# A list scheduler for the middle of a three-stage kernel: gated linear attention, then two feed-forward layers

## The chip, the cores and the metric

The kernel runs on one core of a Trainium2 chip. A core has TensorE (PE in the profile, its weight loads PEld), VectorE (DVE), ScalarE (ACT), GpSimd (POOL) and SyncE (SP, which here issues every DMA). Each engine takes its own instructions strictly in the order of its queue and waits for the others by semaphores. The metric is the time of one execution on the device in microseconds; lower is better.

## The reference

Three stages follow each other; the output of one is the input of the next.

```python
# 1: attention, 4 batches x 8 heads, 768 tokens, head size 48
state = f[t][:, None] * state + outer(k[t], v[t])      # f = sigmoid(f_logit)
y[t] = q[t] @ state
# 2: x is y as 3072 tokens x 384
h = x @ w_in                                           # 384 -> 2048
x = (h * sigmoid(1.702 * h)) @ w_out                   # 2048 -> 384
# 3: four experts, each 384 -> 1024 -> 384
p = probs / (probs.sum(-1) + 1e-9)
out = sum(p[:, e] * (maximum(x @ w1[e], 0) @ w2[e]) for e in range(4))
```

All of it is float32. The kernel reaches this with products of split numbers: a number is a rounded part ("hi", type fp32r) and the rest ("lo", its low half), and hi x hi + hi x lo + lo x hi are summed, so each product is three matmuls.

## The kernel before, in words

**Attention** goes in 24 chunks of 128 tokens (`attend`, line 521). For a chunk DVE, POOL and ACT make the forget gates (tanh, then a scaling, "g"), two scans over time on DVE (lines 547 and 553), and scaled k and q; PE transposes k (line 563), multiplies k by q (scores, line 569), updates the state (line 598) and makes outputs (line 637); masks are applied to the scores (lines 582 and 587).

**The first MoE** (stage 2) goes in 6 blocks of 512 tokens; block j needs the chunks 4j to 4j+3. A block has 16 steps, one for 128 of the 2048 inner columns. Step part L is 9 matmuls (line 679), then come tanh on ACT (685), the gelu product on DVE (687), the hi copy on ACT (469) and the low half on DVE or POOL (471); part M is 9 matmuls of the second product (697) into three banks that collect the whole block, two steps behind L. At the end of a block its sums are taken out of the banks (`sums_out`) and stored to `ydram`.

**The second MoE** (stage 3) uses a fast bilinear scheme, on blocks of 3x3 tiles of x and of w1: `FORM_Y` gives 15 sums of blocks of x, `FORM_W` 15 sums of w1 blocks, and `FORM_H` puts 15 products together. It goes in 32 units n (16 blocks of the experts' inner columns, for each half of the tokens); a unit has 15 products (`p_task`, line 1076) and then, two units later in PE's order, 9 second products U with w2 (`u_task`, line 1116), whose results are multiplied by p on DVE (1129) and added up on POOL (1131).

The weights of stage 3 are prepared during stage 2. `w_forms` loads a 128x1536 block of w1, makes 12 sums on POOL (777) and 15 hi and low halves (786 to 790), and stores them to `wfd`, one 256-column piece per store (794). `w2_piece` loads a third of a w2 block, splits it on ACT (808) and POOL (809) and stores both halves to `w2d` (810, 811). The second MoE loads them back from `wfd` and `w2d`.

**What sets the order.** There are three regimes. `startup` (attention of the chunks 0 to 11 and blocks 0 and 1, with the split of w_in and w_out) follows a list written out by hand, `ORDER`. The loop from line 1291 on (blocks 2 to 4, chunks 12 to 23, all `w_forms` and `w2_piece`) hands out its instructions step by step from a table, `at(i, fn)`, and is outside `manual_schedule`, so that the program's own scheduler may move instructions on the queues; in the trace the first w1 load is issued at 155.83 us, inside the startup. The last block and the second MoE go through `Plan`: each piece of work is a `Task` with an engine, an estimated duration and a delay until others see its result; PE's tasks run in the order of their `place`, and on the other engines, SP included, `order` picks again and again the task that can begin first by these estimates. Buffers come from pools (`F`, `W1`, `W2`, `G`, `S`, `Y`, `TM`, ...), and a task that needs one begins when a slot is free.

## Time and profile before

| | us |
|---|---|
| median of 3 runs (1334.80 to 1340.93) | 1338.81 |
| the profiled execution | 1339.19 |
| its span, first to last instruction | 1337.5 |
| PE busy | 1249.2 (93%) |
| DVE busy | 975.6 (73%) |
| POOL busy | 691.2 (52%) |
| ACT busy | 515.5 (39%) |

"Busy" is the time that an engine's own records cover. PE's matmuls overlap one another, so a busy PE can still run below its best pace; PEclk is the clock granted to it, as a share of 2.4 GHz. The mean over the span is 0.971.

### The profile page before, as it was taken

The page shows a single profiled execution, that of the slowest core. Times are in us where ns is not written, and L with a number is a line of the kernel's source. Part 1 is how long each engine was busy: PE and PEld are TensorE (multiplying, and loading weights), DVE is VectorE, ACT ScalarE, POOL GpSimd, SP SyncE. Part 2 cuts the span into 40 slices and gives each one's busy share as a digit, 9 for nine tenths or more (in the row PEclk, how much of TensorE's full clock was granted, in tenths as well). Part 3 has the DMA queues.
Part 4 walks back from the last instruction along what each step waited for, and adds up shares of the span by engine and source line. Part 5 has one row for each costly group of instructions (what it writes and reads, how often), then busy time and mean ns, then how long its engine had stood idle before and what let it go on. Part 6 is the DMA issues. An engine that isn't in the chain of part 4 may idle for free.

```text
span 1337.5 us, 20734 instructions
## 1 busy us (share of the span) xinstructions
PE 1249.2 (93%) x7470; PEld 1026.9 (77%) x7470; DVE 975.6 (73%) x1443; ACT 515.5 (39%) x967; POOL 691.2 (52%) x591
## 2 busy tenths in 40 slices
PE   6699999987987889899999999999999999999988
PEld 5698877766866767687888888888778888888877
DVE  7989757776767655857777777778977777777774
ACT  4576634444444443333232323233332323232322
POOL 5857434553345442700888555555515555555542
PEclk6899999999989989899999999999999999999989
DMA  6654326776766668144767344436773444353473
GB/s 189 177 149 135 106 92 186 237 245 186 239 211 198 216 196 302 52 154 140 254 207 230 120 129 137 131 121 200 185 194 121 141 130 141 108 159 112 132 154 108
DMA packets 158657, 221.51 MB, mean 166 GB/s; under 512 B 49776, under 2 KB 100048, under 8 KB 158544
## 3 DMA queue, kind: packets, MB, share of 16 engines
q1 hardware_dynamic: 158544, 220.09, 53.7%
q8 instruction: 60, 0.98, 0.3%
q14 instruction: 53, 0.43, 0.1%
HBM read 158.91 MB, written 61.13 MB: 165 GB/s over the span
## 4 chain that ended last, share of the span: by engine, by line
PE 66%; DVE 11%; DMA 10%; issue 5%; POOL 5%; ACT 2%; SPq 1%; DVEq 0%; ACTq 0%; POOLq 0%
PE bank L1116 25%; PE bank L1076 23%; PE bank L697 6%; PE bank L679 5%; DMA wfd<-cv 3%; PE bank L1166 2%; POOL wide L777 2%; PE bank L893 1%; PE bank L637 1%; DMA cv<-in_w 1%; DVE cv L787 1%; DVE arena L553 1%; DMA w2d<-cv 1%; PE bank L569 1%; DVE r L938 1%
## 5 line engine op out<-in xcount | busy, mean ns | idle before, releaser
L1131 POOL TENSOR_TENSOR arena<-arena 128x512 f32<-128x512 f32 x252 | 358.9, 1428 | 270.9 <-DVE arena L1129 270.3
L1076 PE MATMUL bank<-r,r 128*128 128x512 f32 x1440 | 376.9, 391 | 9.9 <-DVE arena L1093 8.2
L1076 PEld LDWEIGHTS bank<-r,r 128*128 128x128 f32 x1440 | 269.9, 188 | 69.9 <-DVE arena L1093 11.9
L1116 PE MATMUL bank<-r,r 128*128 128x512 f32 x876 | 273.9, 389 | 0.0
L1129 DVE TENSOR_TENSOR arena<-bank,cv 128x512 f32<-128x512 f32 x252 | 173.2, 688 | 112.4 <-PE bank L1116 106.7
L1116 PE MATMUL bank<-g,r 128*128 128x512 f32 x744 | 242.9, 389 | 0.0
L679 PE MATMUL bank<-r,r 128*128 128x512 f32 (+1 forms) x792 | 190.5, 386 | 20.0 <-DVE arena L687 19.2
L1116 PEld LDWEIGHTS bank<-r,r 128*128 128x128 f32 x876 | 164.7, 188 | 34.4
L697 PE MATMUL bank<-g,r 128*128 128x512 f32 (+1 forms) x774 | 181.7, 379 | 7.7 <-ACT cv L708 5.2
L679 PEld LDWEIGHTS bank<-r,r 128*128 128x128 f32 x792 | 140.8, 194 | 52.4 <-DVE arena L687 22.8
L697 PEld LDWEIGHTS bank<-g,r 128*128 128x128 f32 x774 | 138.5, 193 | 37.4 <-ACT cv L708 6.0
L1116 PEld LDWEIGHTS bank<-g,r 128*128 128x128 f32 x744 | 139.8, 188 | 29.1
L1093 DVE TENSOR_TENSOR arena<-arena,bank 128x512 f32<-128x512 f32 x192 | 130.1, 683 | 31.4 <-ACT arena L1089 22.8
L1089 ACT ACTIVATE arena<-bank 128x512 f32<-128x512 f32 x101 | 60.4, 598 | 108.6 <-PE bank L1076 107.8
L1100 ACT ACTIVATE r<-arena 128x512 fp32r<-128x512 f32 x75 | 47.1, 632 | 131.7 <-DVE arena L1093 131.7
L777 POOL TENSOR_TENSOR wide<-wide 128x256 f32<-128x256 f32 x64 | 54.9, 874 | 59.0 <-DMA wide<-in_w 33.4
L687 DVE SCALAR_TENSOR_TENSOR arena<-arena,bank 128x512 f32<-128x512 f32 (+1 forms) x88 | 54.9, 626 | 33.1 <-ACT arena L685 30.9
L1093 DVE TENSOR_TENSOR wide<-wide,bank 128x512 f32<-128x512 f32 x96 | 65.6, 683 | 17.7 <-ACT wide L1089 12.2
L469 ACT CAST g<-arena 128x512 fp32r<-128x512 f32 (+1 forms) x88 | 50.9, 581 | 63.4 <-DVE arena L687 62.9
L471 DVE TENSOR_TENSOR g<-arena,g 128x512 fp32r<-128x512 f32 (+1 forms) x66 | 57.5, 871 | 22.9 <-ACT g L469 22.2
L809 POOL TENSOR_TENSOR cv<-cv,cv 128x512 f32<-128x512 f32 x24 | 33.0, 1375 | 73.0 <-ACT cv L808 59.7
L787 DVE TENSOR_TENSOR cv<-wide,cv 128x256 f32<-128x256 f32 x72 | 41.4, 584 | 33.3 <-ACT cv L786 33.1
(140 smaller groups left out, 1562.8 us busy)
## 6 DMA issues: line engine op xcount, KB each, us to landing
r<-wfd SPq DMA_DIRECT2D x160, 384.0 KB, 3.1
wfd<-cv SPq DMA_DIRECT2D x120, 256.0 KB, 2.7
r<-w2d SPq DMA_DIRECT2D x64, 384.0 KB, 4.1
w2d<-cv SPq DMA_DIRECT2D x48, 256.0 KB, 2.3
wide<-ydram SPq DMA_DIRECT2D x38, 256.0 KB, 4.1
arena<-in_qkf SPq DMA_DIRECT2D x48, 192.0 KB, 4.3
arena<-in_v SPq DMA_DIRECT2D x24, 256.0 KB, 4.2
wide<-in_w_in SPq DMA_DIRECT2D x12, 512.0 KB, 3.7
```

The source lines that it names most:

```text
L471: eng.tensor_tensor(out=lo, in0=src, in1=hi.bitcast(F32), op=ALU.subtract)
L679: nc.tensor.matmul(h, w[:, c0:c0 + 128], x[:, 512 * k + t0:512 * k + t0 + n], start=(i == 0), stop=(i == 8),)
L687: nc.vector.scalar_tensor_tensor(out=gf, in0=th, scalar=1.0, in1=h, op0=ALU.add, op1=ALU.mult)
L697: nc.tensor.matmul(bank[d][:, t0:t0 + n], w[:, c0:c0 + 128], g, start=(f == fs[0] and i == 0 and t0 == 0), stop=(f == fs[-1] and i == 2 an ...
L777: nc.gpsimd.tensor_tensor(out=t, in0=have[a], in1=have[b], op=ALU.add if sg > 0 else ALU.subtract)
L787: nc.vector.tensor_tensor(out=lo, in0=fv, in1=hl[:, :, 0], op=ALU.subtract)
L1076: nc.tensor.matmul(bk.ap, a, y.ap, start=(r == chain[0] and m == 0), stop=(m == 2), skip_group_check=True,)
L1089: P.task("ACT", act, lambda: nc.scalar.activation(out=b.ap, in_=bk.ap, func=ACTF.Copy, scale=float(sign)), [bk], [b])
L1093: P.task("DVE", dve, lambda: nc.vector.tensor_tensor(out=b.ap, in0=b.ap, in1=bk.ap, op=ALU.add if sign > 0 else ALU.subtract), [b, bk], [b])
L1116: nc.tensor.matmul(bk.ap, w.ap[:, c0:c0 + 128], g[f][y].ap, start=(m == 0), stop=(m == 5))
L1129: P.task("DVE", dve, lambda: nc.vector.tensor_tensor(out=m.ap, in0=bk.ap, in1=pb.ap, op=ALU.mult), [bk, pb], [m])
L1131: P.task("POOL", pool, lambda: nc.gpsimd.tensor_tensor(out=a.ap, in0=a.ap, in1=m.ap, op=ALU.add), [a, m], [a])
```

## The change

Four things are done together.

1. `Plan` also takes blocks 2 to 4, the chunks 12 to 23, the w1 sums, the experts' probabilities and the test of the decay (`guard`). The table `at`, `w2_piece` and the unplanned loop go. In the plan a chunk starts with step i (`chunk_steps`: 0, 3, 6, 10, ... 42); PE makes its transposes and scores after the L of step i+3, its update and outputs after that of step i+4 (one later still for the first chunk). The w1 blocks start at the steps `w_at`: 2, 7, 13, 19, 25, 30, 36, 42.
2. The scheduler is extended. A task may have several ways (`other`): the low half of a step, k and q of a chunk and the positive w1 low halves can go to DVE or POOL, and the second way is taken when it would end no later by the estimates. Tasks have a `rank` that decides between tasks that can begin at the same time (w1 work has 2). Pools hold places made of cells, so that one piece of memory can serve several pools. All masks of chunks 12 to 23 become an ACT copy and a POOL select; in the kernel before they are one DVE product each.
3. The w1 halves of three forms are collected in one tile of 1536 columns (`WG`, two of them), and each tile goes out in two stores of 384 KB (80 stores in all; 120 of 256 KB before).
4. w2 is not split in stage 2 and `w2d` is gone. `load_w2` reads two 128x384 pieces of w2 for each unit into slots of the pool `Y` and splits them on ACT and POOL, beside the unit's products.

The memory for the gates, `FG`, moves to the end of the arena, the block sums of blocks 2 to 4 go through the pool `TM` (the slots of tanh and gelu product), and the terms of `later_forms` are loaded one by one, each after its own mark.

```diff
+                for w in t.ways:
+                    known = max([d.end + (d.late if d.engine != w[0] else 0.0) for d in t.deps], default=0.0)
+                    begin = max(known, free.get(w[0], 0.0), place)
+                    if w is not t.ways[0] and begin + w[1] > max(known, free.get(t.ways[0][0], 0.0), place) + t.ways[0][1]:
+                        continue
+                    key = begin, t.rank, known, t.n
...
-        P.pool("S", [*(asl(i) for i in range(9, 14)), slot(0), slot(1), slot(2)], free=6.0)
-        P.pool("Y", [slot(3), slot(4), slot(5)])
-        P.pool("TM", [asl(i) for i in range(14, 18)])
+        P.pool("S", [*(a_slot(i) for i in range(9, 12)), *(b_slot(i) for i in range(5))])
+        P.pool("TM", [a_slot(i) for i in range(12, 16)])
+        P.pool("WT", [b_slot(3 + i // 2, i % 2) for i in range(6)])
+        P.pool("Y", [b_slot(5), b_slot(12), b_slot(13)])
+        P.pool("WG", [(CV3[i], [("b", 6 + 3 * i + x // 2, x % 2) for x in range(6)]) for i in range(2)])
...
+            P.task("POOL", 1.4, lambda: nc.gpsimd.tensor_tensor(out=t[:, 2], in0=t[:, 2], in1=pc, op=ALU.mult), [Q, PCB], [Q],
+                   other=[("DVE", 0.85, lambda: nc.vector.tensor_tensor(out=t[:, 2], in0=t[:, 2], in1=pc, op=ALU.mult))])
...
+                P.task("ACT", 0.62, lambda g=g, dst=dst: nc.scalar.copy(
+                    out=dst, in_=sb[g].ap.rearrange("p (h t) -> p h t", h=4)), [sb[g]], [am_b[g]])
+                P.task("POOL", 1.1, cover, [am_b[g]], [am_b[g]])
...
-            P.task("DVE", dve, lambda: nc.vector.tensor_tensor(
-                out=lo.ap, in0=gf.ap, in1=hi.ap.bitcast(F32), op=ALU.subtract), [gf, hi], [lo])
+            P.task("DVE", 0.8, lambda: nc.vector.tensor_tensor(
+                out=lo.ap, in0=gf.ap, in1=hi.ap.bitcast(F32), op=ALU.subtract), [gf, hi], [lo],
+                other=[("POOL", 1.5, lambda: nc.gpsimd.tensor_tensor(
+                    out=lo.ap, in0=gf.ap, in1=hi.ap.bitcast(F32), op=ALU.subtract))])
...
+                    P.task("ACT", 0.42, hi, [bs], [h], rank=2)
+                    P.task("DVE", 0.53, lo, [bs, h], [l], rank=2, other=[
+                        ("POOL", 0.95, lambda lo=lo: lo(eng=nc.gpsimd))] if sign > 0 else ())
+                for i in range(2):
+                    stored["w", 2 * u + i, g] = dma(393216, lambda i=i, g=g, tile=tile: [(
+                        wfd[2 * u + i, g], tile.ap[:, 768 * i:768 * i + 768])], parts)
...
+        for i in range(n_last + 16):
+            s, place = early + i, 10.0 * i - 1e6
+            l_task(s, place)
+            wait.append(s)
+            if i in chunk_steps:
+                x = 1 if i == 0 else 0
+                going[i] = att_task(chunk_steps[i], [place + 32 + 10 * x, place + 42 + 10 * x, place + 43 + 10 * x])
...
+            if i in w_at:
+                w_forms(w_at[i], [P.te[-1][2]] if i > 2 else [])
...
+            if len(wait) > 2:
+                m = wait.pop(0)
+                m_task(m, place + 5)
+                if m % 16 == (early + 15) % 16 and m < early + n_last + 15:
+                    sums((m - early) // 16 + 2)
+        attended = next(t for t in reversed(P.tasks) if t in x_b[1][0][3].writers)
...
         for k, t in need:
-            y_load(raws[k, t], t, k)
+            y_load(raws[k, t], t, k, [attended])
...
-                    b.ap.bitcast(F32)[:, 768 * x:768 * x + 768].rearrange("p (f c) -> p f c", f=2),
-                    w2d[u, x].rearrange("p (f i c) -> p i f c", f=2, i=2)[:, i],
-                ) for x in range(2)]
-            dma(786432, go, (), [b], after)
+            for f in range(2):
+                r = Buf("Y")
+                f0 = DM * (2 * f + i)
+                after = [dma(196608, lambda r=r, f0=f0: [(r.ap[:, 0:DM], w2[u][:, f0:f0 + DM])], (), [r],
+                             [*after, *last2])]
+                last2[:] = after
+                h, l = (lambda f=f, x=x: b.ap[:, 768 * x + DM * f:768 * x + DM * f + DM] for x in range(2))
+                P.task("ACT", 0.48, lambda r=r, h=h: nc.scalar.copy(out=h(), in_=r.ap[:, 0:DM]), [r], [hi])
+                P.task("POOL", 1.15, lambda r=r, h=h, l=l: nc.gpsimd.tensor_tensor(
+                    out=l(), in0=r.ap[:, 0:DM], in1=h().bitcast(F32), op=ALU.subtract), [r, hi], [lo])
...
-                later_forms([marks[x // 2 + 2, 7 * (x % 2)] for x in range(20)])
+                later_forms([marks[x // 2 + 1, 7 * (x % 2)] for x in range(22)])
...
-        for i in range(e):
-            for fn in side.pop(i, []):
-                fn()
-            L1(early + i)
-            if len(pend) > 2:
-                L2()
-        plan = second_moe()
-        done = plan.order()
+        done = second_moe().order()
         with tc.manual_schedule():
             for t in done:
                 t.fn()
```

## Rows read from the trace of the kernel before

**Rows 1.** Page, part 2: busy tenths of PE in 40 slices of 33.4 us.

```profile
PE   6699999987987889899999999999999999999988
```

**Rows 2.** Windows by stage: length, busy us by engine, PEclk, DMA share, GB/s.

```profile
200.00:222.29 22.29, 19.45 (x224) 15.27 (x224) 20.02 (x32) 11.56 (x25) 12.79 (x15) 1.00 0.52 161
222.29:515.86 293.57, 255.02 (x2033) 203.20 (x2032) 198.63 (x324) 132.89 (x291) 131.22 (x149) 0.95 0.70 221
515.86:601.08 85.22, 78.52 (x326) 62.09 (x325) 55.05 (x69) 30.22 (x53) 30.98 (x21) 0.96 0.43 147
601.08:920.00 318.92, 318.48 (x1402) 262.70 (x1401) 237.44 (x343) 96.56 (x159) 187.96 (x134) 1.00 0.52 166
920.00:1000.00 80.00, 75.80 (x327) 60.47 (x326) 72.01 (x104) 31.00 (x53) 30.59 (x21) 1.00 0.71 184
```

**Rows 3.** Timeline of PE, 438 to 453 us: start, duration, instructions.

```profile
438.13 2.21 PE L679 MATMUL bank<-r,r 128*128 128x512 f32 x9
440.18 2.21 PE L697 MATMUL bank<-g,r 128*128 128x512 f32 x9
...
452.34 0.85 PE L697 MATMUL bank<-g,r 128*128 128x512 f32 x3
```

**Rows 4.** Lines, 222 to 516 us: count, busy us, mean ns, idle before.

```profile
L679 PE MATMUL bank<-r,r 128*128 128x512 f32 x432 | 115.0, 412 | 17.6 <-DVE arena L687 17.6
L697 PE MATMUL bank<-g,r 128*128 128x512 f32 x416 | 107.0, 400 | 7.7 <-ACT cv L708 5.2 <-DVE cv L706 0.8 <-DVE g L471 0.8
...
L809 POOL TENSOR_TENSOR cv<-cv,cv 128x512 f32<-128x512 f32 x23 | 31.1, 1353 | 72.1 <-ACT cv L808 58.9 <-DMA arena<-in_qkf 6.7 <-DMA wfd<-cv 6.6
```

**Rows 5.** Waits, 222 to 516 us: who for whom, total, times, longest.

```profile
PE bank L679 <- DVE arena L687: 17.6, 8, 5.9
...
PE bank L637 <- DVE arena L587: 8.5, 5, 2.9
```

**Rows 6.** Timeline of all engines, 376 to 385 us.

```profile
377.99 0.62 POOL L538 TENSOR_SCALAR arena<-arena 128x512 f32<-128x512 f32 x1
...
379.05 1.26 POOL L809 TENSOR_TENSOR cv<-cv,cv 128x512 f32<-128x512 f32 x1
...
379.22 2.17 DVE L547 TENSOR_TENSOR_SCAN arena<-arena,floor 128x512 f32<-128x512 f32 x1
...
383.18 0.67 DVE L687 SCALAR_TENSOR_TENSOR arena<-arena,bank 128x512 f32<-128x512 f32 x1
...
383.91 1.65 PE L679 MATMUL bank<-r,r 128*128 128x512 f32 x3 [5.88 <-DVE arena L687]
```

**Rows 7.** Timeline of POOL and DVE, 549 to 558 us.

```profile
549.80 1.74 POOL L959 TENSOR_TENSOR wide<-arena 128x512 f32<-128x512 f32 x1
550.32 1.77 DVE L938 TENSOR_TENSOR r<-arena,r 128x512 fp32r<-128x512 f32 x1
...
551.50 1.74 POOL L959 TENSOR_TENSOR arena<-arena 128x512 f32<-128x512 f32 x1
```

**Rows 8.** Line 471, DVE, 222 to 516 us: ns min/median/max.

```profile
L471 DVE TENSOR_TENSOR g<-arena,g x47: 675/693/1786, 227.8 to 515.0; 128x512 fp32r<-128x512 f32 x47
```

**Rows 9.** Line 1131 on POOL, whole span: ns min/median/max.

```profile
L1131 POOL TENSOR_TENSOR arena<-arena x252: 1277/1295/1759, 640.2 to 1299.6; 128x512 f32<-128x512 f32 x126
```

**Rows 10.** Line 1180 on POOL, the same columns.

```profile
L1180 POOL TENSOR_TENSOR arena<-arena x9: 1011/1017/1062, 1298.6 to 1318.2; 128x384 f32<-128x384 f32 x9
```

**Rows 11.** Page, part 6: DMA issues, KB each, median us to landing.

```profile
wfd<-cv SPq DMA_DIRECT2D x120, 256.0 KB, 2.7
...
arena<-in_qkf SPq DMA_DIRECT2D x48, 192.0 KB, 4.3
```

**Rows 12.** Chain that ended last, 516 to 560 us: start, us, what.

```profile
519.68 5.08 DMA arena<-ydram
...
524.78 5.38 DMA arena<-ydram
...
530.23 6.61 DMA ydram<-arena
```

More of the change, by code (lines that the diff above doesn't have):

```diff
@@ L98, with __init__ @@
 class Buf:
[L99 to L100 removed]
+    def __init__(self, pool=None, whole=None):
+        self.pool, self.place, self.whole = pool, None, whole
         self.writers, self.readers, self.refs = [], [], []
+        self.left, self.till = 0, 0.0
     @property
     def ap(self):
[L105 to L117 removed]
+        return (self.whole or self).place[0]
 class Task:
[L121 to L122 removed]
+    def __init__(self, ways, late, deps, rank):
+        self.ways, self.late, self.deps, self.rank = ways, late, deps, rank
+        self.engine, self.us, self.fn = ways[0]
         self.begin = self.end = None
@@ L129, in __init__, with pool, hold, at @@
     def __init__(self):
-        self.tasks, self.pools, self.te = [], {}, []
-    def pool(self, name, aps, free=0.0):
-        self.pools[name] = [Slot(a, free) for a in aps]
-    def hold(self, name, slots, buf):
-        for i in slots:
-            self.pools[name][i].held = buf
-        buf.slot = self.pools[name][slots[0]]
-        return buf
-    def task(self, engine, us, fn, reads=(), writes=(), after=(), late=0.1, place=None):
+        self.tasks, self.pools, self.te, self.holds = [], {}, [], {}
+    def pool(self, name, places):
+        self.pools[name] = places
+    def hold(self, buf, cells, ap=None):
+        for c in cells:
+            self.holds[c] = buf
+        buf.place = ap, cells
+        return buf
+    def at(self, place):
+        t = 0.0
+        for c in place[1]:
+            b = self.holds.get(c)
+            if b is not None:
+                if b.left:
+                    return None
+                t = max(t, b.till)
+        return t
+    def task(self, engine, us, fn, reads=(), writes=(), after=(), late=0.1, place=None, rank=0, other=()):
         deps = list(after)
@@ L146, in task @@
             deps += b.readers + b.writers
-        t = Task(engine, us, late, fn, list(dict.fromkeys(deps)))
-        t.bufs = list(dict.fromkeys(list(writes) + list(reads)))
+        t = Task([(engine, us, fn), *other], late, list(dict.fromkeys(deps)), rank)
+        t.bufs = list(dict.fromkeys(b.whole or b for b in [*writes, *reads]))
         for b in writes:
@@ L169, in order @@
                 d.users.append(t)
-        ready = {t.engine: [] for t in self.tasks}
         for t in self.tasks:
-            if not t.left and t.engine != "PE":
-                ready[t.engine].append(t)
+            for b in t.bufs:
+                b.left += 1
+        ready = [t for t in self.tasks if not t.left and t.engine != "PE"]
         done, k = [], 0
@@ L189, in order @@
             if best is None:
                 raise ValueError("no task can begin")
-            (begin, _, _), t = best
+            (begin, _, _, _), t, (t.engine, t.us, t.fn) = best
             for b in t.bufs:
-                if b.slot is None:
-                    free_slots = [s for s in self.pools[b.pool] if s.at() is not None]
-                    s = min(free_slots, key=lambda s: s.at())
-                    s.free, s.held = s.at(), b
-                    b.slot = s
+                if b.place is None:
+                    open_ = [p for p in self.pools[b.pool] if self.at(p) is not None]
+                    self.hold(b, (p := min(open_, key=self.at))[1], p[0])
@@ L198, in order @@
             t.begin, t.end = begin, begin + t.us
+            for b in t.bufs:
+                b.left -= 1
+                b.till = max(b.till, t.end + t.late)
             free[t.engine] = t.end
@@ L202, in order @@
             else:
[L203 removed]
+                ready.remove(t)
             done.append(t)
@@ L842, in second_moe, with r_part, a_slot, b_slot @@
-        old = {r: P.hold(*held(r), Buf(held(r)[0])) for r in range(20) if r not in (16, 17)}
+        def r_part(r, n, i):
+            w = 1536 // n
+            return R[r][:, w * i:w * i + w], [("r", r, x) for x in range(6 // n * i, 6 // n * (i + 1))]
+        def a_slot(i):
+            return asl(i), [("a", i)]
+        def b_slot(i, h=None):
+            if h is None:
+                return slot(i), [("b", i, 0), ("b", i, 1)]
+            return slot(i)[:, 256 * h:256 * h + 256], [("b", i, h)]
@@ L948, in y_load @@
             rows = yrows[j]
+            after = [*after, *(stored[r, k] for r in rows if (r, k) in stored)]
             dma(262144, lambda: [(buf.ap, ydram[rows[0], k])], (), [buf], after)
```

468 lines of the change are left out of this document (266 added, 202 removed).

## The prediction, made before the change was run

> **What bounds the kernel now.** The profiled execution took 1339.19 us (span 1337.5 and 1.7 around it), 0.4 above the median of the three runs, 1338.81; the sum below is made on the span and put on 1339.2. I read the page's forty slices first. TensorE is busy in nine tenths of nearly every slice, but slices 8 to 16 fall to seven or eight [rows 1]. The windows by stage turn this into places: from 601 to 920 us, the second MoE under its planner, PE is busy 318.48 of 318.92 us at full clock, so an order there can give nothing; from 222.29 to 515.86, blocks 2 to 4 with attention and the w1 sums beside them, 255.02 of 293.57, at a mean clock of 0.95; from 515.86 to 601.08, the planned last block, 78.52 of 85.22 [rows 2].
>
> Busy is not pace, so I price PE's work by distances between starts. A group of nine matmuls follows another after 2.04 us. From 438.13 to 452.34 PE did five groups and one whole chunk of attention (transposes, scores, state update, outputs) with no stall: 14.21 less 5 x 2.04 leaves 4.0 us a chunk [rows 3]. Between 222.29 and 515.86 stand 48 first-product groups and 46 second-product groups [rows 4] and chunks 12 to 23, two of them without a state update (0.45 each): 94 x 2.04 + 12 x 4.0 - 0.9 + 0.5 for two small transposes = 239.4 us. The stage took 293.6, so it **loses 54.2**. From 515.86 to 601.08 there are 34 groups and 18 product matmuls (about 4.4 us): 73.8 of 85.2, a **loss of 11.4**. Together 65.6 us, 45.3 of it idle PE and the rest groups at a lower clock; this is all that ordering can return.
>
> Why it loses: PE waits for the gelu product on DVE (L687, 17.6 us in 8 waits, the longest 5.9) and for masks on DVE (L587) [rows 5]. One of them in time: POOL does the gate of a chunk at 377.99, behind two w1 sums; POOL then splits w2 at 379.05, and the DVE scan of 379.22, which had to wait for the gate, is stretched to 2.17; the gelu product that PE needs stands behind it on DVE and runs at 383.18, PE at 383.91 after 5.88 us idle [rows 6]. That is a matter of queue order, not of a full engine: DVE is busy 198.6 and POOL 131.2 of 293.6 us [rows 2].
>
> **The change, part by part.** *Queue order in blocks 2 to 5.* All 64 steps, twelve chunks, eight w1 blocks and the sums go through the list scheduler. PE's order is written out: transposes and scores of a chunk stand three steps after its start instead of two, updates and outputs together a step later, so DVE's chain of scans has about a step (4.1 us) more. All the other queues are filled by who can begin first. The instructions that PE runs are the same, so its floor stays 239.4 + 73.8. What stays lost is the question, and the trace has two planned stages for it: 0.1% (601 to 920) and 13% (11.4 of 85.2). On 239.4 us these are 0.3 and 32. The mix here has the scans and POOL work which the first lacks, and less than the burst of the second; I take **20**, somewhat above the middle, for the reason in the next paragraph.
>
> *The pair DVE and POOL.* 24 masks go from DVE to ACT and POOL, and the low halves may go to POOL. Against it stands how they run together: from 549.80 to 551.50 each POOL operation starts 1.70 after the one before, one DVE operation between, and both take 1.7 [rows 7], while the same DVE operation alone takes 0.69 [rows 8] and POOL's 1.29 [rows 9]: 1.70 is 0.86 of the sum, so they run nearly one after the other. I add up what has two operands in SBUF on DVE and all of POOL, at undisturbed durations x 0.86 (small shapes estimated by width from these rows): 48 low halves 28, scans and k of 12 chunks 35, 120 w1 halves 42, 96 w1 sums 62, POOL's five parts of 12 chunks 39: 206 of 239 us, 86%. That is below PE, but not far; moving 10 low halves adds 5. Hence 20 and not 10. The Trainium skill states this as a rule (SBUF — State Buffer, "Who interferes with whom": a DVE instruction with two SBUF inputs and a GpSimd one that reads SBUF shut each other out for a whole instruction), and Perfetto Trace Analysis, "Optimizing Scalar/DVE Operations", adds that offloading between those two might not help. By that the offload is worth nothing or less; the first rival below is what it would do here.
>
> *w2's split.* Out of the stage go 24 loads, 24 ACT casts, 24 POOL subtracts (33 us busy, mean 1.35 [rows 4]) and 48 stores from SP; that gain is inside the 54.2. Into each of the 32 units of the second MoE come two 192 KB loads in place of two of 384 KB, two ACT casts and two POOL subtracts of 1.01 [rows 10]. A unit is 99 matmuls, 22.5 us; POOL goes from 59% busy [rows 2] to 68%. Queued behind a waiting subtract is the next accumulator addition (L1131), and for that waits, much later, only the scratch slot of a product. U needs w2 a whole unit after its slot comes free, some 22 us, for two loads (under 5 us each) and 3 us of work, so the cover is wide. The three Y slots are shared with the second half's forms around 920 to 1000, where 4.2 us are lost already. Bounds: 0 (601 to 920) to 4.2 again; I take **2**.
>
> *Stores of the w1 forms.* 120 stores of 256 KB, 2.7 us to landing [rows 11], become 80 of 384 KB, each from a tile of six 256-column parts, in two buffers. Same bytes; SP has 40 issues less. Who waits for a landing is the ACT cast that first writes the tile again, and behind it on ACT stands a step's tanh. The order books 4.0 us for it (2.2 + 393216/220000 in the code). No cost at 2.7; it is the slower rival.
>
> *The start.* The w1 work no longer runs inside the first stage's tail: from 200 to 222.29 PE is busy 19.45 of 22.29 with DVE at 20.02 [rows 2]. Its return lies between 0 and 2.8 of idle PE, a little more through the clock; I take **3**. The other way, loads of chunk 12 now queue on SP behind the stores of the last early sums. PE first asks for that chunk after seven groups, 14.3 us; loads 4.3 [rows 11], gate 0.6, two scans of at most 2.2 [rows 6] and four short operations under 0.7 are 12.1. Hidden by 2 us; if not, it costs those few. So 0.
>
> *The sums of a block* now use the slots of the steps' own tanh and product, and those wait for the stores. In the planned stage of before this is seen: two loads of 5.08 and 5.38, a store of 6.61, then the gelu product, which came free only by that store [rows 12]. Three times a block ends; with quiet queues two groups cover a store, so I add **1** in the first region and leave the last region's loss at **11**, since the loads of the first forms (now held until the last chunk) again meet the sums' stores of block 4.
>
> Sum: 1339.2 - 65.6 - 3 + 20 + 1 + 11 + 2 = 1304.6; **about 1304 us**.
>
> **Rivals.** *A, the pair becomes the bound.* If the 86% cannot be packed, as from 540 on, the stage loses 13% (32) and w1 work spills into the last block, whose loss doubles to 22: 1339.2 - 65.6 - 3 + 32 + 1 + 22 + 2 = 1327.6. For it: DVE operations at 1.7 next to POOL's. Against it: most of the work here is no such burst, and w2's subtracts leave. Chance 0.18.
>
> *B, slower: ACT stands behind a store.* Forty tiles are filled in two buffers. If a store lands 6.6 us after issue, as in [rows 12], and not in 4.0, an ACT cast at the queue's head waits 2.6, the tanh behind it too, and the PE group after that. A step's two groups of slack hide one such wait, not a series. The gain of 35 is gone at 0.9 us of PE per tile; at 1.3 (half of the 2.6) the time is 1304 + 52 = 1356. For it: landings of 5 to 6.6 when loads crowd. Against it: 2.7 is the median in this very stage, and w2's 19 MB leave it. Chance 0.09.
>
> *C, U waits for w2's low half.* The split is done beside the products instead of ahead; if planned and real POOL times differ so that each of 32 units waits 0.5 us, that is 16: 1320. Against it the 22 us of cover. It lies inside the forecast's own range.
>
> *D, little changes:* stalls only move from the gelu product to other waits, with 55 or more still lost, about 1335. Chance 0.04. *Better than forecast:* losses of 5 and 5 instead of 20 and 11: 1283 and below. Chance 0.08.
>
> **How the numbers follow.** The forecast, 1304, with its own range of 1285 to 1320, has 0.61. Range for 8 in 10: down to 1280 (nearly all stalls gone) and up to 1334 (A, losing 38 us there instead of 32); left out are B, D's upper half and the best part of "better". About 0.5%, 6.7 us, is what a measurement of this kernel can tell from no change: faster has 0.61 + 0.08 + 0.18, less 0.01 for A's worst, = 0.86; same 0.05 (D and that); slower 0.09 (B).
>
> **What would show it.** In the new profile the stretch from the first group of block 2 to the end of the last block should be near 345 us against 379, with no wait of PE above 3 us and the clock at 1.00 in nearly all of it; the gelu product should start within 1 us of tanh. PE should stay over 99% busy in the units of the second MoE. DVE and POOL together should rise in that stretch. A is right if low halves of 1.7 us fill DVE and PE waits for them; B, if ACT's idle time ahead of the w1 casts is ended by wfd stores and PE waits for tanh; C, if PE waits for POOL subtracts at U. I am wrong if the idle time in that stretch is still above 50 us.

## The result and the profile after

The changed kernel takes 1294.70 us (median of four runs, 1291.54 to 1295.61); the kernel before, run beside it, 1339.87 (1334.80 to 1341.16). The ratio is 0.9665, with a 95% interval of 0.9635 to 0.9696: 45 us faster. The forecast of 1304 was 9 us too long; the range and the sign held. The steps behind the number held less well.

The page of the changed kernel, its part 2 (PE in 40 slices of 32.3 us); it answers to [rows 1]:

```profile
span 1293.9 us, 20638 instructions
...
PE   5699999999999987999999999999999999999988
```

The long shallow dip of before is gone. One short dip is left, around 455 to 515 us. The same in windows by stage, with the stages cut at the same PE instructions as in [rows 2] (the first group of block 2; the first group of the last block, 48 steps later; the first product matmuls that have PE to themselves, after the last group of that block):

```profile
200.00:219.72 19.72, 19.72 (x227) 15.58 (x226) 10.27 (x18) 8.05 (x17) 4.04 (x5) 1.00 0.29 81
219.72:470.63 250.91, 248.51 (x2033) 202.23 (x2031) 191.77 (x284) 131.65 (x298) 173.02 (x199) 0.99 0.57 194
470.63:560.32 89.69, 75.95 (x326) 61.88 (x325) 51.16 (x69) 32.78 (x60) 36.27 (x26) 0.92 0.38 136
560.32:880.00 319.68, 319.24 (x1407) 263.81 (x1406) 236.19 (x345) 109.50 (x187) 219.00 (x160) 1.00 0.49 149
880.00:960.00 80.00, 77.81 (x339) 63.10 (x339) 70.39 (x106) 35.07 (x62) 42.70 (x30) 1.00 0.72 189
```

Against before, by length: the part up to the first group of block 2 is 2.6 us shorter (219.72 against 222.29); blocks 2 to 4 take 250.9 in place of 293.6 (-42.7); the last block, block 5, 89.7 in place of 85.2 (+4.5); the second MoE 733.6 in place of 736.4 (-2.8). The sum, -43.6, is the difference of the spans, 1337.5 and 1293.9.

The waits of PE from 219 to 562 us (who for whom, total, times, longest) answer to [rows 5]. Eight waits for the gelu product and five for masks have become one long wait and four short ones:

```profile
PE bank L982 <- ACT g L967: 13.7, 1, 13.7
PE bank L924 <- POOL arena L872: 1.8, 2, 1.5
...
```

How the long one comes about is seen in the timeline of all engines, 468 to 495 us (line 1069 is the hi copy of a w1 sum and 1070 its low half, 962 tanh, 964 the gelu product, 967 and 968 the step's hi and low half, 997 and 994 take a block's sums out of the banks, 1127, 1143 and 1149 work for the second MoE's first forms, 787 any DMA):

```profile
468.71 3.11 SPq L787 DMA_DIRECT2D arena<-ydram  x6
...
478.14 0.95 SPq L787 DMA_DIRECT2D wfd<-cv  x2
...
484.69 0.40 ACT L1069 CAST cv<-wide 128x256 fp32r<-128x256 f32 x1 [9.48 <-DMA wfd<-cv]
485.00 0.59 ACT L962 ACTIVATE arena<-bank 128x512 f32<-128x512 f32 x1
485.13 0.43 DVE L1070 TENSOR_TENSOR cv<-wide,cv 128x256 f32<-128x256 f32 x1 [9.11 <-ACT cv L1069]
...
488.30 1.74 DVE L968 TENSOR_TENSOR g<-arena,g 128x512 fp32r<-128x512 f32 x1
...
489.45 3.37 POOL L1143 TENSOR_TENSOR arena<-arena,wide 128x512 f32<-128x512 f32 x2
489.96 1.75 DVE L1127 TENSOR_TENSOR r<-arena,r 128x512 fp32r<-128x512 f32 x1
491.63 1.74 DVE L1149 TENSOR_TENSOR arena<-arena 128x512 f32<-128x512 f32 x1
...
493.30 0.68 DVE L964 SCALAR_TENSOR_TENSOR arena<-arena,bank 128x512 f32<-128x512 f32 x1
...
493.90 1.27 DVE L997 TENSOR_SCALAR arena<-bank 128x512 f32<-128x512 f32 x2
494.01 0.62 ACT L967 CAST g<-arena 128x512 fp32r<-128x512 f32 x1 [6.03 <-DVE arena L964]
```

The second of the two stores in the chain that ended last (start, us, what), and PE's timeline from 494 us on:

```profile
478.77 5.82 DMA wfd<-cv
```

```profile
494.72 4.05 PE L982 MATMUL bank<-g,r 128*128 128x512 f32 x9 [13.73 <-ACT g L967]
```

The loads for the first forms fill the transfers. The stores of 478.14 and 478.77 stand among them, and the second lands at 484.59; until 484.69 ACT stands behind it with a w1 copy at the head of its queue and tanh, long ready, behind that. DVE stands for the same time at that copy's low half (line 1070), which waits for ACT. Then DVE and POOL alternate at 1.7 us, as in [rows 7], and DVE comes to line 997 only at 493.90. The profile puts PE's wait down to the hi copy of line 967, which ended last (494.63). By the program the waiting product is the first of the last block: its own hi copy ran at 486.34, and what it lacks is the first bank, which line 997 empties at about 494.5. So the wait is for block 4's sums. Their banks were complete at about 479, but in DVE's queue they stand behind the w1 low half and all that became late with tanh. Windows over that stretch (length, busy us of PE, PEld, DVE, ACT, POOL, clock, DMA share, GB/s):

```profile
480.00:485.00 5.00, 0.99 (x5) 0.49 (x3) 0.00 (x0) 0.31 (x1) 3.17 (x3) 0.98 1.03 401
485.00:490.00 5.00, 0.00 (x0) 0.00 (x0) 4.80 (x6) 2.82 (x7) 4.65 (x4) 0.50 0.45 143
490.00:495.00 5.00, 0.28 (x1) 0.29 (x1) 5.00 (x6) 0.99 (x2) 5.00 (x4) 0.50 0.54 211
```

First DVE does nothing and the transfers run at 401 GB/s; then DVE and POOL are full and the transfers are half empty. PE's last matmul before the wait ends at 480.99; from 485 to 495 us its granted clock is 0.50, which is 1.2 GHz, and the group after the wait takes 4.05 us in place of 2.2.

One row says against the forecast that PE's own work grew. PE's timeline, 283 to 305 us (answers to [rows 3]):

```profile
283.41 2.21 PE L956 MATMUL bank<-r,r 128*128 128x512 f32 x9
...
285.99 1.71 PE L863 MATMUL bank<-arena 48*128 48x128 f32 x16
...
304.27 1.07 PE L956 MATMUL bank<-r,r 128*128 128x512 f32 x4
```

From 283.41 to 304.27 stand eight groups and one whole chunk without a stall: 20.86 - 8 x 2.04 = 4.54 us for a chunk, where before it was 4.0. The scores of a chunk, eight matmuls of the program that the profile records as 16, take 1.71 us. The row of the kernel before that stands between those of [rows 3]:

```profile
442.75 1.16 PE L569 MATMUL bank<-arena 48*128 48x128 f32 x16
```

### The profile page after: what moved, and what is told of

It reads as the page before. It is cut to its first block, busy times and chain, and to the rows that moved or that the text cites. A ratio compares the mean times of both kernels' runs of the same rounds, so it can differ in the third digit from the quotient of the medians.

```text
span 1293.9 us, 20638 instructions
## 1 busy us (share of the span) xinstructions
PE 1240.5 (96%) x7470; PEld 1028.1 (79%) x7470; DVE 949.6 (73%) x1387; ACT 540.2 (42%) x1029; POOL 791.4 (61%) x689
## 4 chain that ended last, share of the span: by engine, by line
PE 84%; DVE 5%; DMA 4%; POOL 3%; issue 2%; ACT 1%; SPq 1%; DVEq 0%; POOLq 0%; ACTq 0%
PE bank L1303 26%; PE bank L1263 24%; PE bank L982 8%; PE bank L956 7%; PE bank L712 5%; PE bank L694 5%; PE bank L1353 2%; DMA wfd<-cv 1%; PE bank L863 1%; PE bank L924 1%; PE bank L584 1%; PE bank L652 1%; POOL wide L1051 1%; DMA wide<-ydram 1%; SPq L787 1%
## 5 line engine op out<-in xcount | busy, mean ns | idle before, releaser
L1263 PE MATMUL bank<-r,r 128*128 128x512 f32 x1440 | 375.9, 391 | 7.5 <-DVE wide L1280 6.9
L1303 PE MATMUL bank<-r,r 128*128 128x512 f32 x879 | 275.7, 390 | 0.0
L1303 PE MATMUL bank<-g,r 128*128 128x512 f32 x741 | 242.5, 390 | 0.0
L982 PE MATMUL bank<-g,r 128*128 128x512 f32 x576 | 147.3, 401 | 13.7 <-ACT g L967 13.7
L1280 DVE TENSOR_TENSOR wide<-wide,bank 128x512 f32<-128x512 f32 x191 | 129.4, 682 | 28.1 <-ACT wide L1276 24.0
L956 PE MATMUL bank<-r,r 128*128 128x512 f32 x576 | 140.9, 390 | 0.1
L982 PEld LDWEIGHTS bank<-g,r 128*128 128x128 f32 x576 | 107.7, 191 | 40.6 <-ACT g L967 14.1
L1287 ACT ACTIVATE r<-wide 128x512 fp32r<-128x512 f32 x77 | 48.3, 633 | 130.5 <-DVE wide L1280 130.4
L1276 ACT ACTIVATE wide<-bank 128x512 f32<-128x512 f32 x101 | 60.4, 598 | 92.5 <-PE bank L1263 91.7
L1280 DVE TENSOR_TENSOR arena<-arena,bank 128x512 f32<-128x512 f32 x97 | 66.2, 683 | 21.9 <-ACT arena L1276 14.8
L694 PE MATMUL bank<-r,r 128*128 128x512 f32 (+1 forms) x360 | 76.0, 357 | 2.4 <-DVE arena L702 1.5
L712 PE MATMUL bank<-g,r 128*128 128x512 f32 (+1 forms) x360 | 74.8, 353 | 0.0
L968 DVE TENSOR_TENSOR g<-arena,g 128x512 fp32r<-128x512 f32 x59 | 50.7, 859 | 31.4 <-ACT g L967 31.1
L964 DVE SCALAR_TENSOR_TENSOR arena<-arena,bank 128x512 f32<-128x512 f32 x64 | 43.3, 677 | 29.2 <-ACT arena L962 27.6
```

What stands on the lines that cost most here:

```text
L694: nc.tensor.matmul(h, w[:, c0:c0 + 128], x[:, 512 * k + t0:512 * k + t0 + n], start=(i == 0), stop=(i == 8),)
L712: nc.tensor.matmul(bank[d][:, t0:t0 + n], w[:, c0:c0 + 128], g, start=(f == fs[0] and i == 0 and t0 == 0), stop=(f == fs[-1] and i == 2 an ...
L956: nc.tensor.matmul(hb.ap, w[:, c0:c0 + 128], x[:, 512 * k:512 * k + 512], start=(i == 0), stop=(i == 8))
L968: P.task("DVE", 0.8, lambda: nc.vector.tensor_tensor(out=lo.ap, in0=gf.ap, in1=hi.ap.bitcast(F32), op=ALU.subtract), [gf, hi], [lo], other ...
L982: nc.tensor.matmul(bank[d], w[:, c0:c0 + 128], g.ap, start=(f == fs[0] and i == 0), stop=(f == fs[-1] and i == 2),)
L1263: nc.tensor.matmul(bk.ap, a, y.ap, start=(r == chain[0] and m == 0), stop=(m == 2), skip_group_check=True,)
```

## The experiments

Each was run beside the kernel before on the same chip; "ratio" is to that. Where a run gains or loses is seen in the lengths of its stages in us, each from one profiled execution and cut at the same PE instructions. The changed kernel and a_yload issue the same instructions in the same order, and so do a_scores and a_both: these pairs differ by up to 1.4 us in a stage, so less than that says nothing. The profiled execution of b_w2 was its longest, 1307.38 us.

| | to block 2 | blocks 2 to 4 | last block | second MoE |
|---|---|---|---|---|
| kernel before | 222.3 | 293.6 | 85.2 | 736.4 |
| b_w2 | 221.7 | 269.4 | 75.6 | 739.0 |
| b_nosub | 221.0 | 275.8 | 80.3 | 736.8 |
| b_noload | 224.6 | 280.6 | 76.7 | 737.4 |
| changed kernel | 219.7 | 250.9 | 89.7 | 733.6 |
| a_yload | 218.4 | 249.6 | 90.1 | 732.2 |
| a_w2in | 219.6 | 252.3 | 98.8 | 751.7 |
| a_scores | 219.5 | 247.9 | 85.3 | 734.1 |
| a_both | 219.8 | 247.8 | 84.5 | 733.0 |
| a_late | 219.3 | 248.1 | 91.3 | 732.9 |
| a_shared | 220.9 | 245.7 | 83.2 | 732.7 |
| a_dve | 219.4 | 245.7 | 81.4 | 733.3 |
| a_mask | 220.0 | 248.9 | 91.9 | 733.9 |
| a_lead | 220.2 | 259.3 | 84.2 | 733.6 |

**Which part of the change gives the gain.** b_w2 is the kernel before with the fourth part of the change alone:

```diff
-  work.append(forms[3*i:3*i+3] + (pieces[i//2:i//2+1] if i % 2 == 0 else []))
+  work.append(forms[3*i:3*i+3])          # w2_piece and w2d go
   ...                                    # load_w2 as in the changed kernel, but both halves of a tile are marked as one
```

> The kernel before with one part of the change alone: w2 is split beside the products of the second MoE, and the splits of w2 leave blocks 2 to 4, whose order is otherwise untouched. Theory (the gain is queue order): a gain of 5 to 15 us, 1325 to 1334, since the gelu product still stands behind the scans and w1 work. Rival (the gain is the lighter stage: 33 us of POOL, 15 of ACT and 19 MB less): most of the 45 us, 1310 or less.

Measured: 1303.01 us, ratio 0.9747 (0.9729 to 0.9765). So 33.5 of the 45 us come with w2's split alone, under the old order of queues; the rest, some 11 us, is what the other three parts bring together. I had put the gain on the order. Blocks 2 to 4 and the last block of b_w2, then PE's waits in blocks 2 to 4:

```profile
221.67:491.05 269.38, 248.28 (x2032) 201.23 (x2031) 195.38 (x326) 123.29 (x272) 104.34 (x130) 0.96 0.59 190
491.05:566.61 75.56, 74.82 (x327) 60.61 (x326) 51.01 (x67) 31.52 (x57) 32.78 (x24) 1.00 0.29 100
```

```profile
PE bank L678 <- DVE arena L686: 15.4, 3, 6.0
PE bank L636 <- DVE arena L586: 3.5, 3, 2.3
```

By stage the 11 us are a difference of larger numbers. In blocks 2 to 4, w2's removal gives 24.2 us and the other parts 18.5 more (269.4 to 250.9). In the last block, w2's removal gives 9.7, and the new order takes that back and 4.5 more (75.6 to 89.7). So ordering did help where I looked for it, and lost most of it one stage later. PE is idle 21.1 us in blocks 2 to 4 of b_w2, against 38.6 [rows 2]. Its waits for the gelu product are three in place of eight, but in sum 15.4 us in place of 17.6 [rows 5]; what shrank more are other waits.

**What in w2's split cost it.** Two kernels leave out one piece of that work each; what they leave out is in their expectations.

```diff
 # b_nosub
-  nc.gpsimd.tensor_tensor(out=r, in0=r, in1=h, op=ALU.subtract)
 # b_noload
-  nc.sync.dma_start(out=r, in_=w2[u][:, cs])
```

> The kernel before without the POOL subtract of w2's split in the stage (the low half is stored as the unsplit copy, so the output's low part is wrong in value; loads, ACT casts and both stores stay). Theory 1, POOL's time is what w2 cost (24 subtracts, 33 us busy, next to the chunks' gate and masks): most of the 33.5 us that moving the whole split gave returns, 1305 to 1315, and the long waits of PE for the gelu product (17.6 us in 8) fall below 8. Theory 2, what w2 cost is ACT and POOL standing at the head of their queues for the 256 KB load: 1325 to 1337, since the ACT cast still waits for it. Theory 3, the bytes and the raw tiles (stores of 19 MB): also 1325 to 1337; the next kernel parts theory 2 from 3.

> The kernel before without the 24 loads of w2 in the stage (the split is done on whatever the tile holds, so those values are wrong; casts, subtracts and 48 stores stay). Theory 2, waits for the load at the head of ACT and POOL: 1308 to 1320. Theory 1, POOL's time: within 6 us of before, 1330 to 1337. Theory 3, bytes and raw tiles: a third of w2's transfers go, so some 5 to 12 us: 1325 to 1332.

Measured: without the POOL subtract 1315.75, ratio 0.9853 (0.9821 to 0.9885), 19.6 us by the ratio; without the load 1321.96, 0.9909 (0.9880 to 0.9939), 12.2 us. Neither theory takes all: b_nosub ends just outside the first one's 1305 to 1315, b_noload between the bands of the second and the third. Together, 31.8, they come near what the whole move gives, 33.8 by its ratio; but that is no proof that they add, since in blocks 2 to 4 alone they give 17.7 and 12.9, more than the 24.2 of the whole move. What w2's stores and tiles cost by themselves was not run. PE's waits in the two from 222.29 to 515.86 us, b_nosub first (for the gelu product 17.6 in 8 before [rows 5]):

```profile
PE bank L679 <- DVE arena L687: 10.8, 6, 4.6
```

```profile
PE bank L679 <- DVE arena L687: 16.6, 5, 4.3
...
PE bank L637 <- DVE arena L587: 3.6, 4, 1.5
...
PE bank L697 <- ACT cv L708: 1.0, 1, 1.0
```

Without the subtract that wait falls, though not below 8 as the first theory had it; without the load it stays, and the waits for masks (8.5 before [rows 5]) and for ACT's part of a block's sums (5.2 before [rows 4]) fall in its place. In b_w2, where both are gone, the waits for the gelu product are back at 15.4. Waits move when the queues change, so no one of them can be charged to one piece.

**Would the list scheduler have carried w2's work?** a_w2in splits w2 once more in the changed kernel's stage:

```diff
+ def w2_piece(u, n, after):
+     tile = Buf("WG")                    # one of the two wide tiles
+     r, h = Buf(whole=tile), Buf(whole=tile)
+     ...                                 # load, ACT cast, POOL subtract (rank 2), two stores
```

> The changed kernel with w2's split done once more in the stage, planned by the list scheduler (24 loads of 256 KB, 24 ACT casts, 24 POOL subtracts, 48 stores, in the same two wide tiles as the w1 forms); the second MoE stays as in the changed kernel and doesn't read it. Theory, the lighter stage makes the gain and any order pays for w2 there: slower by 20 to 33 us than the changed kernel, 1313 to 1328. Rival, the scheduler would have packed it (PE idles 18 us there now, POOL 178 of 261 us busy): at most 8 us slower, up to 1303.

Measured: 1325.21, ratio 0.9919 (0.9894 to 0.9943): 31 us over the changed kernel, as the theory had it, but not where it had it. Blocks 2 to 4 stay fed (252.3 us, and PE busy 256.89 of 260.28 us up to 480); the last block is 9 us longer and the second MoE 18. The w1 work is pushed out instead: its hi copies (line 1083 here, 1069 in the changed kernel, where the last starts at 485.8) run on to 603.6 us, and behind their stores come the loads of w2 for the second products, so that PE waits 16.16 us. Lines of a_w2in: the group of the copies (ns min/median/max, first and last start), then the timeline of all engines:

```profile
L1083 ACT CAST cv<-wide x72: 387/403/419, 243.1 to 603.6; 128x256 fp32r<-128x256 f32 x72
```

```profile
594.97 0.51 ACT L1225 CAST r<-ends 128x384 fp32r<-128x384 f32 x1 [5.18 <-DMA ends<-in_w]
...
595.54 0.80 PE L1319 MATMUL bank<-g,r 128*128 128x512 f32 x1 [16.16 <-ACT r L1225]
```

Here 24 of the 64 fills of two tiles are w2's, so a shortage of tiles would explain it; that is not shown, since w2 with tiles of its own was not run. What follows is narrower than the theory: with the tiles that the change leaves, w2 doesn't fit beside w1, while in the second MoE its split costs the changed kernel nothing that can be seen (733.6 us against 736.4 before).

**The scores.** a_scores puts the old order of the 16 score matmuls back:

```diff
- for r in range(2):
-     def score(r=r):
-         for p in range(4): ...          # four of one row half, then four of the other
+ def score():
+     for h in range(8):
+         p, r = h // 2, h % 2            # row halves by turns
```

> The changed kernel with one edit: the eight score matmuls of a chunk alternate between the two heads of a pair (rows 0 to 47 and 64 to 111 of the array) as they did in the kernel before, in one PE task instead of two. Theory: the sixteen passes take 1.16 us so and 1.71 grouped by half; PE is the bound in that stretch, so 12 chunks give back 12 x 0.55 = 6.6 us: about 1288 against 1294.7. Rival: the masks and ACT copies after the scores are the bound, PE then waits there and the time stays at 1294.

Measured: 1286.94, ratio 0.9622 (0.9605 to 0.9639), and in PE's timeline the 16 take 1.16 again:

```profile
288.23 1.16 PE L863 MATMUL bank<-arena 48*128 48x128 f32 x16
```

Twelve chunks times 0.55 are 6.6 us; 1294.70 less 1286.94 is 7.8. That the two agree is in part chance: blocks 2 to 4 are only 3.0 us shorter and the last block 4.4. PE's waits of a_scores, 219 to 480 us and 480 to 562 us:

```profile
PE bank L924 <- POOL arena L872: 3.9, 9, 1.1
```

```profile
PE bank L982 <- ACT g L967: 8.0, 1, 8.0
```

Part of what the scores return is lost again to waits for masks (3.9 us, 1.8 before the edit), as the rival had it; and in the order that the planner made with the new score task the long wait came out at 8.0 us in place of 13.7.

The Trainium skill gives a reason for the two durations (TensorE: Matmul & The Clock Gate, "The mechanism"): a weight load runs beside a matmul in flight only when their row groups differ. The trace fits that as far as it goes: in either order the matmuls of one row half start some 111 ns apart, and by turns those of the two halves start 7 ns apart, side by side. Since the end of a matmul is modelled, the records don't show whether the weight load is what sets the 111 ns.

**The long wait.** Three edits on the loads of the first forms (`y_load`). a_yload holds them until a named store of the last w1 block is issued; a_both does that on top of a_scores:

```diff
- y_load(raws[k, t], t, k, [attended])
+ y_load(raws[k, t], t, k, [attended, stored["w", 2 * NU - 1, 4]])
```

> The changed kernel with one edit: the 21 loads of the first forms may be issued only after the last store of w1 forms is issued, instead of after the last attention chunk. Theory: the one long PE wait (13.7 us at 481 us, and about 2 us at the lower clock behind it) comes from ACT, whose head copy waits for a w1 store that is queued on SP and lands late among those loads; with the store ahead of them it goes: 1279 to 1283. Rival: it is the burst of DVE and POOL work of the first forms that blocks the gelu product; then the wait only comes later, with a time of 1290 to 1296.

> Both edits together on the changed kernel. If each theory holds, the gains add: 1294.7 - 6.6 - 14 = about 1274. If PE is not the bound around the scores, the same as the second edit alone, about 1281.

Measured: 1294.15, ratio 0.9688 (0.9673 to 0.9703), and 1287.68, 0.9635 (0.9618 to 0.9653). Both missed their aim: tiles of a block don't finish in the order of their numbers, the store named is not the last, and the order came out as it was. The first stands as a second measurement of the changed kernel, the second as one of a_scores.

a_late waits for all five stores of that block, with the scores by turns:

```diff
+ y_load(raws[k, t], t, k, [attended, *(stored["w", 2 * NU - 1, g] for g in range(5))])
```

> The changed kernel with scores alternating the row halves again, and the 21 loads for the first forms held until all five stores of the last w1 block are issued (the earlier form of this edit changed nothing in the order). Theory, the store that ACT stood behind (13.7 us of idle PE) was late because of those loads: against the version with the scores alone (1286.9) 6 to 12 us less, 1275 to 1281, and no PE wait over 4 us between 450 and 520. Rival, the loads are only moved and the forms are late at the start of the second MoE: 1285 to 1292, with the PE idle between 520 and 570 instead.

Measured: 1293.69, ratio 0.9683 (0.9662 to 0.9705): some 7 us slower than a_scores, and PE's longest wait is 7.7 us where a_scores has 8.0. The theory that it was that store falls as far as this: with the store out of the way, the same thing happens behind the loads themselves. Timeline of all engines in a_late, 476 to 486 us (1126 and 1127 are hi copy and low half of a form):

```profile
479.50 0.62 ACT L1126 CAST r<-arena 128x512 fp32r<-128x512 f32 x1 [2.57 <-DMA arena<-ydram]
...
483.38 0.62 ACT L1126 CAST r<-arena 128x512 fp32r<-128x512 f32 x1 [3.26 <-DMA arena<-ydram]
483.90 0.61 ACT L967 CAST g<-arena 128x512 fp32r<-128x512 f32 x1
484.03 0.69 DVE L1127 TENSOR_TENSOR r<-arena,r 128x512 fp32r<-128x512 f32 x1 [3.19 <-ACT r L1126]
...
484.63 1.28 DVE L997 TENSOR_SCALAR arena<-bank 128x512 f32<-128x512 f32 x2
...
485.47 4.18 PE L982 MATMUL bank<-g,r 128*128 128x512 f32 x9 [7.73 <-DVE arena L997]
```

ACT waits at 1126 for a load, DVE at 1127 for ACT, and behind DVE's head stands line 997, for which PE waits. The step's hi copy at 483.90 needs a gelu product that ran at 477.07; it too waits only for its place in a queue.

What looks common to both is that the planner expects a transfer sooner than it comes. a_shared changes that and nothing else against a_scores:

```diff
+ if t.nbytes:
+     free["Q"] = max(free.get("Q", 0.0), t.end) + t.nbytes / 400e3
+     t.late = max(t.late, free["Q"] - t.end + 1.9)
```

> The changed kernel with scores alternating the row halves, and with one more rule in the planner: a transfer's landing is booked behind the bytes of the transfers issued before it, at 400 GB/s (the rate that the trace of the changed kernel shows from 475 to 485 us), and no longer at a fixed 3.4 to 4.0 us after its issue. Theory: the long PE stall near 480 comes from an order that books landings too early in the burst of loads for the first forms, so that an ACT instruction at the head of its queue waits for a transfer with tanh or the gelu copy behind it; booked later, those stand behind the step's own work: 1276 to 1282 against 1286.9 with the scores alone, and no PE wait over 4 us between 450 and 520. Rival: the work due there (last sums of w1, first forms, 21 loads) is too much for DVE, POOL or the transfers in any order: the loss comes back as other waits and the time is 1285 to 1291.

Measured: 1284.13, ratio 0.9610 (0.9581 to 0.9639). By time it can't be told from a_scores, nearer to the rival's band than to the theory's, so that early landings were what cost the time is argued and not shown. PE's longest wait is 5.5 us in place of 8.0, and a transfer has the smaller part in it: tanh at 487.92 waits 2.21 us for a store, then the gelu product, ready at 488.5, starts at 490.85, behind an addition and a low half for the forms of 1.75 and 1.74 on DVE, each beside an addition on POOL:

```profile
487.92 0.60 ACT L968 ACTIVATE arena<-bank 128x512 f32<-128x512 f32 x1 [2.21 <-DMA ydram<-arena]
...
490.85 1.47 DVE L970 SCALAR_TENSOR_TENSOR arena<-arena,bank 128x512 f32<-128x512 f32 x2
```

a_dve keeps the edits of a_scores and a_shared and puts those additions on DVE alone:

```diff
- combine(("DVE", "POOL")[turn % 2], f, src, raws[k, t], ts[0][2], sg)
+ combine("DVE", f, src, raws[k, t], ts[0][2], sg)
  ...                                     # and the additions in y_load of the first forms
```

> The version before (alternating scores, landings booked behind the bytes ahead) with the additions for the second MoE's first forms and for the loads that they sum all on DVE; there they stood on DVE and POOL by turns. Theory, the pair: from 474 to 500 us its POOL additions of 1.7 (1.28 alone) and DVE additions of 1.76 (0.68 alone) run one after the other, the gelu product and the low halves of the last steps among them (1.76 in place of 0.69), so that two engines do less than DVE alone would: with DVE alone the wait of 5.5 us and the slow clock after it go, and the DVE additions take 0.7: 1274 to 1281 against 1284.1. Rival: 27 more additions of 0.69 (19 us) fill DVE in a stretch of some 40 us that already holds the last steps' and the forms' work, and the gelu product waits behind them: 1284 to 1292.

Measured: 1281.53 (1279.65 to 1282.38), ratio 0.9585 (0.9572 to 0.9598): faster than a_scores, half a microsecond past the theory's band, and with an interval that overlaps a_shared's. The rows are plainer than the time. The additions in a_shared (line 1155; ns min/median/max), then in a_dve (line 1156):

```profile
L1155 POOL TENSOR_TENSOR wide<-arena x5: 1289/1732/1742, 476.5 to 496.6; 128x512 f32<-128x512 f32 x5
L1155 DVE TENSOR_TENSOR wide<-wide,arena x5: 679/1746/1766, 477.8 to 500.6; 128x512 f32<-128x512 f32 x5
```

```profile
L1156 DVE TENSOR_TENSOR wide<-wide,arena x8: 676/680/1770, 478.6 to 499.9; 128x512 f32<-128x512 f32 x8
```

One addition of 1.74 on each engine by turns is slower than two of 0.68 on one of them. That is the rule that I cited from the Trainium skill (SBUF — State Buffer, "Who interferes with whom"), and here it costs time: the windows of 480 to 570 us, PE's busy time and clock, in a_scores, a_shared and a_dve:

```profile
480.00:570.00 90.00, 83.64 (x352) 67.48 (x353) 62.96 (x81) 36.44 (x65) 32.78 (x23) 0.94 0.37 125
```

```profile
480.00:570.00 90.00, 82.88 (x353) 66.31 (x352) 62.00 (x79) 35.11 (x62) 27.89 (x20) 0.96 0.37 126
```

```profile
480.00:570.00 90.00, 86.73 (x371) 69.89 (x371) 59.51 (x90) 34.28 (x60) 9.98 (x8) 0.98 0.37 123
```

With all three edits together a_dve beats the changed kernel by 0.8% (0.9585 against 0.9665, intervals apart). PE's longest wait in it is 2.4 us.

**Masks and lead.** Two parts of the new order, undone one at a time in the changed kernel:

```diff
 # a_mask: per half g
- P.task("ACT", 0.62, ... copy ...); P.task("POOL", 1.1, cover, ...)
+ P.task("DVE", 0.7, ... tensor_tensor(..., in1=mask, op=ALU.mult), [sb[g]], [am_b[g]])
 # a_lead
- att_task(..., [place + 32 + 10*x, place + 42 + 10*x, place + 43 + 10*x])
+ att_task(..., [place + 22 + 10*x, place + 32 + 10*x, place + 33 + 10*x])
```

> The changed kernel with the 24 causal masks as one product on DVE each, as before the change, in place of an ACT copy and a POOL select. Theory: masks on DVE stand in the chain of scans and gelu products, which cost PE 4 to 6 us of waits before; moving them off is worth 2 to 8 us, so this is 1297 to 1303. Rival: with DVE busy 194 of 261 us the 17 us fit, and POOL (178 of 261) and ACT are relieved: 1290 to 1296.

> The changed kernel with attention on PE one step earlier again (transposes and scores two steps after the chunk's start, updates and outputs three), as before the change. Theory: the longer lead is what lets the scheduled stage run almost without idle PE, since DVE's chain of scans takes over two steps: some 0.5 to 1.5 us of PE for each of 12 chunks, 1301 to 1313. Rival: the scheduler fits the chain into the shorter lead: 1292 to 1298.

Measured: a_mask 1296.53, ratio 0.9709 (0.9683 to 0.9735), which overlaps the changed kernel's interval, so where the masks run is not shown to matter; a_lead 1299.23, 0.9727 (0.9700 to 0.9753), just clear of it, 4.5 us by the medians and 8 by the ratios: between the two bands. By stage the theory is right where it looks: with the shorter lead blocks 2 to 4 take 259.3 us in place of 250.9, some 0.7 us a chunk. The last block is 5.5 us shorter (84.2 against 89.7): the order came out without the long wait, and none there is above 3 us.

## Why the prediction was right in size and wrong in parts

**Start, -3:** measured -2.6. Right.

**Floor of 239.4 + 73.8 unchanged:** failed. "The instructions that PE runs are the same" holds for their number, not for their order: the scores by half add 12 x 0.55 = 6.6 us of PE's time, of which undoing them gave 3.0 back in this stage. I had a duration for every operation of a chunk and did not ask which of PE's neighbours it depended on, although the diff shows the loop turned round.

**20 us stay lost in blocks 2 to 4, +1 for the sums:** measured 250.9 - 239.4 = 11.5, of which 6.6 are the scores, so stalls and slow clock keep 5. The choice of 20 "and not 10" for the pair at 86% load was too careful. The pair did not bind there: the low half on DVE has a median of 0.695 us in the whole region, as in [rows 8], and only 5 of 64 went to POOL, not 10. That 11.5 came no further from 20 is luck in part: the stalls were a quarter of what I gave them, and the scores, for which I gave nothing, took up the rest. Rival A was right about the mechanism in one place, the burst after 485 us, and about no other.

**Last region 11:** measured 15.9. Rival B's mechanism happened all along and cost PE once. In blocks 2 to 4 ACT waited for `wfd` stores ahead of w1 copies again and again, and no wait of PE came of it; ACT's waits from 219.72 to 470.63 us:

```profile
ACT cv L1069 <- DMA wfd<-cv: 17.3, 13, 2.8
```

In the burst it then stood 9.48 us behind one, and "no wait of PE above 3 us" was wrong by 10.7. The forecast that the last region would keep its loss "since the loads of the first forms again meet the sums' stores" named the right burst; what those loads met first was the last w1 block's stores, which the copy at the head of ACT's queue was waiting for, and behind that stood the taking out of block 4's sums. Nor was the loss of 11.4 before a fixed price of that block: in b_w2, with the old order and without w2's split, it is 75.6 - 73.8 = 1.8. Why that order meets the same loads so cheaply was not looked into.

**Second MoE +2:** measured -2.8. The cover of a unit was as wide as worked out: PE 319.24 of 319.68 us busy, and no wait for a POOL subtract (rival C); from 880 to 960 it loses 2.2 us where 4.2 went before [rows 2].

With these the sum closes: 1304.6 + 0.4 (start) - 9.5 (21 to 11.5) + 4.9 (11 to 15.9) - 4.8 (second MoE) = 1295.6, as for the profiled execution (span 1293.9 and 1.7 around it). Of the signs, the stretch of both stages took 340.6 us where 345 was forecast, with 16.1 of it idle.

**The cause of the 54.2 us.** This is where the reading failed most, though the sum doesn't show it. I read [rows 5, 6] as "a matter of queue order, not of a full engine" and left w2's removal inside that number without a price of its own. Under the old order it alone returns 24.2 of the 54.2, and 33.5 in the whole kernel; order and the rest return another 18.5 of the 54.2. The rows had a sign of it: [rows 6] has POOL's split of w2 at 379.05, just ahead of the scan that it stretches, and [rows 4] has 58.9 us in which POOL stood at the split waiting for ACT's copy. In queues that run strictly in order, work that waits at the head is a cost of that work, and taking it away can return as much as ordering it.

## What to carry to other kernels

Before pricing a new order, price the old order without the work that is moved out: here that was three quarters of the net gain, and a kernel with that edit alone would have shown it first. Compare runs stage by stage: the new order won 18.5 us in one stage and lost 14.1 in the next, and the total shows neither. A list scheduler needs landing times of the busy moment, not of the quiet one, since tanh or a hi copy stands in ACT's queue behind work that waits for a transfer; booking them later shortened the long wait here, and its gain in time is not shown. And don't alternate additions of two SBUF operands between DVE and POOL to share a burst.

## What was not expected of the hardware

Sixteen matmuls of 48 rows, by the profile's count, take 1.16 us when they alternate between the two row halves and 1.71 when they go half by half, with the same operands. With transfers at 401 GB/s a 384 KB store issued at 478.77 landed at 484.59, 5.8 us later; the median of its kind is 3.6 in the same kernel, and 2.7 for 256 KB in the kernel before [rows 11]. In a_late PE's wait of 7.73 us is followed by nine matmuls that take 4.18 us in place of 2.20, with the granted clock at 0.50 (1.2 GHz) from 485 to 490 us. By the starts of the groups the first two after the wait take 3.97 and 2.86 us in place of 2.04, so the wait cost a third as much again.
